# Moving zero fills on VectorE in a decode block: two attention sum banks behind six products, the output accumulator ahead of the layer norm

## Chip, cores, metric

The kernel runs on one core of a Trainium2 chip. The metric is device time in microseconds (us). Runs are compared with runs of the kernel before on the same chip.

## The reference, cut to what matters

Four sequences, one new token each, width 640. A layer norm feeds two branches that are added to x: attention over the last 2048 positions of a cache with 32 heads of 192, and a gated feed-forward of width 1536.

```python
xn = layernorm(x)
q = xn @ wq                                         # 640 -> 32 x 192
k, v = k_cache[:, :, Sk - W:], v_cache[:, :, Sk - W:]   # W = 2048
p = softmax(q . k * 192 ** -0.5)
attn = (p . v) @ wo
ffn = (silu(xn @ w1) * (xn @ w3)) @ w2
return x + attn + ffn
```

Each element of the cache is used once: 32 K heads and 32 V heads of 3 MB each (3.146 million bytes) are 201 of the 223 MB that are read.

## The kernel before

Positions lie on the partitions. VectorE multiplies a quarter of a K head by q (a "product", `mult`), TensorE sums pieces of it into PSUM (`adder`), VectorE finishes the sum (`reduce_quarter`), and after four quarters a softmax and the product with V (`pv`) follow. K has two buffers and V three; a load is issued when the last user of its buffer is done.

```python
# query projection: two rounds of six PSUM banks, evacuated to qbc
for c0 in range(0, NQ, 6):
    qps = [pool.tile([P, QC], FP32, tag=tag, name="qps")
           for pool, tag in ((ps_add, "ps"), (ps_add, "ps"), (ps_o, "o_ps"), (ps_o, "o_ps"), (ps_m, "mt"), (ps_t, "t"))]
    ...                                   # matmuls, copies by ScalarE, in round one also VectorE

o_banks = []                              # the same two banks, now for the sums with V
for i in range(2):
    o_ps = ps_o.tile([P, 2 * Dh], FP32, tag="o_ps", name="o_ps")
    nc.vector.memset(o_ps[:], 0.0)
    o_banks.append(o_ps)
acc = ps_acc.tile([P, N0], FP32, name="acc")
nc.vector.memset(acc[:], 0.0)
...
def mult(u):                              # quarter g of head h
    h, g = u // GQ, u % GQ
    pr = ppool.tile([P, JQ, Dh], BF16, tag="pr")
    nc.vector.tensor_tensor(out=pr[:], in0=kts[h][:, g * JQ:(g + 1) * JQ, :],
                            in1=qbc[:, h * Dh:(h + 1) * Dh].unsqueeze(1).to_broadcast([P, JQ, Dh]), op=ALU.mult)
...
for h in range(H):                        # slots of the hand-made schedule; add(slot, phase, what)
    if h >= KBUFS:
        add((h - KBUFS + 1) * GQ, 0, load_k, h)
    for u in range(u0, ul + 1):
        add(u, 1, mult, u)
        add(u + 1, 2, adder, u)
        add(u + 1, 8, reduce_quarter, u)
    ...
```

## Time and profile before

| | before |
|---|---|
| median of three runs | 525.47 us (525.42 to 525.69) |
| profiled span | 523.7 us |
| busy: TensorE, VectorE, ScalarE | 69%, 65%, 11% |
| transfers | 222.96 MB read, the 16 engines busy 99.3% |
| first product; third K load issued | 33.24 us; 42.47 us |

The prediction shows the lines for this. One more view belongs to it, the waits of the queue's sequencer (who waited for whom: us in total, times, longest):

```profile
SPq L140 <- DVE pr L292: 316.1, 30, 13.1
SPq L140 <- DMA kt<-in_A_k_cache_dram: 72.4, 25, 5.6
```

A K load waits for VectorE's last product on the same buffer.

### The profile page before, as it was taken

To read this page: it belongs to the slowest core of one execution; us is meant where nothing else is said; L and a number is where in the kernel's file an instruction comes from. 1 tells how busy PE (TensorE), PEld (TensorE's weight loads), DVE (VectorE), ACT (ScalarE), POOL (GpSimd) and SP (SyncE) were. 2 spreads that over 40 slices of the span, in tenths; PEclk is the share of its full clock that TensorE was granted. 3 is DMA by queue.
4 is the path that set the end of the run, shared out by engine and by line. 5 is a ranking of instruction groups with operands and counts; after the bars stand their busy time and mean duration, and the time that the engine had idled before them with its cause. 6 is when DMAs were issued, how large, how long until landed. Compare 5 with 4: busy or idle time off the path is not lost.

```text
span 523.7 us, 4813 instructions
## 1 busy us (share of the span) xinstructions
PE 358.9 (69%) x2337; PEld 74.5 (14%) x1643; DVE 339.2 (65%) x410; ACT 57.3 (11%) x179; POOL 5.6 (1%) x12
## 2 busy tenths in 40 slices
PE   0976756887658776757557768576686876655785
PEld 0100111121111111111111111111111111111122
DVE  3248953687656767577647877467666867667671
ACT  2121111111001110110000111001101100001111
POOL 4000000000000000000000000000000000000000
PEclk9989986898788988799987988799878888999889
DMA  9999999999999999999999999999999999999996
GB/s 391 420 443 421 435 431 428 437 427 429 431 435 428 433 424 445 422 434 432 434 432 433 428 435 434 430 429 432 431 435 432 429 435 430 433 432 429 435 422 276
DMA packets 11904, 223.26 MB, mean 426 GB/s; under 512 B 1332, under 2 KB 1608, under 8 KB 3052
## 3 DMA queue, kind: packets, MB, share of 16 engines
q1 hardware_dynamic: 11868, 222.96, 99.3%
q8 instruction: 15, 0.25, 0.2%
q14 instruction: 5, 0.04, 0.0%
q10 hardware_dynamic: 16, 0.01, 0.0%
HBM read 222.96 MB, written 0.01 MB: 426 GB/s over the span
## 4 chain that ended last, share of the span: by engine, by line
DMA 60%; PE 19%; DVE 15%; ACT 3%; issue 2%; SPq 1%; DVEq 0%
DMA kt<-in_A_k_cache_dram 44%; PE ps L303 11%; DMA w<-in_B_w_dram 10%; DVE pr L292 10%; DMA vt<-in_A_v_cache_dram 5%; PE po L376 4%; DVE sc L311 2%; PE qps L258 2%; ACT ex L339 1%; DVE z L347 1%; DMA x_sb<-in_A_x_dram 1%; PE mt L333 1%; ACT L339 0%; ACT negm L336 0%; PE mt L320 0%
## 5 line engine op out<-in xcount | busy, mean ns | idle before, releaser
L303 PE MATMUL ps<-pr,idb 128*128 128x512 bf16 x768 | 217.3, 426 | 140.5 <-DVE pr L292 140.5
L292 DVE TENSOR_TENSOR pr<-kt,qbc 128x3072 bf16<-128x3072 bf16 x128 | 223.5, 1747 | 101.2 <-DMA kt<-in_A_k_cache_dram 101.2
L311 DVE TENSOR_REDUCE sc<-ps 128x16 f32<-128x512 f32 x128 | 87.1, 681 | 2.7 <-PE ps L303 2.7
L355 PE MATMUL o_ps<-vt,z 128*8 128x384 bf16 x1024 | 53.4, 345 | 0.2 <-DVE z L347 0.2
L376 PE MATMUL po<-o_sb,sel_w 128*32 128x192 f32 x128 | 49.2, 518 | 0.6 <-ACT o_sb L358 0.6
L347 DVE TENSOR_TENSOR z<-ex,mask_b 128x256 bf16<-128x256 bf16 x32 | 13.5, 423 | 41.3 <-ACT ex L339 41.3
L355 PEld LDWEIGHTS <-z 128*8 128x8 bf16 x1024 | 24.5, 89 | 95.2 <-issue 83.5
L358 ACT COPY o_sb<-o_ps 128x384 f32<-128x384 f32 x32 | 15.3, 479 | 189.6 <-PE o_ps L355 189.6
L328 ACT ACTIVATE gneg<-gmax 1x128 f32<-1x128 f32 x32 | 9.8, 308 | 164.6 <-DVE gmax L325 164.6
L320 PEld LDWEIGHTS mt<-idf,lmax 128*1 128x1 f32 x32 | 3.4, 105 | 132.1 <-issue 131.1
L376 PEld LDWEIGHTS po<-o_sb,sel_w 128*32 128x32 f32 x128 | 13.9, 131 | 30.0 <-issue 28.8
L303 PEld LDWEIGHTS <-idb 128*128 128x128 bf16 x124 | 12.0, 96 | 37.7 <-issue 31.6
L333 PEld LDWEIGHTS mt<-ones_ff,gneg 1*128 1x128 f32 x64 | 9.6, 186 | 47.9 <-issue 44.5
L258 PE MATMUL qps<-wt,xnT 128*128 128x512 bf16 x60 | 16.2, 438 | 0.0
L336 ACT COPY negm<-mt 128x1 f32<-128x1 f32 x32 | 5.1, 159 | 72.4 <-PE mt L333 72.4
L333 PE MATMUL mt<-ones_ff,gneg 1*128 1x1 f32 x64 | 12.3, 259 | 0.7 <-ACT gneg L328 0.7
L325 DVE TENSOR_REDUCE gmax<-mt 1x4 f32<-1x128 f32 x32 | 8.8, 275 | 6.0 <-PE mt L320 5.7
L363 PEld LDWEIGHTS po<-rsum,tot_w 128*32 128x32 f32 x64 | 4.4, 108 | 51.0 <-ACT ex L339 34.7
L320 PE MATMUL mt<-idf,lmax 128*1 128x128 f32 x32 | 11.3, 353 | 0.0
L339 ACT ACTIVATE ex<-sc,negm 128x64 bf16<-128x64 f32 x32 | 11.1, 348 | 1.0
L279 PE MATMUL acc<-wo_t,oT 128*4 128x320 bf16 x96 | 9.2, 298 | 1.3 <-DMA wo_t<-in_A_wo_dram 1.3
L214 PE MATMUL xnT_ps<-idb,xn 4*128 4x4 bf16 x5 | 0.4, 178 | 13.5 <-DVE xn L209 13.5
(74 smaller groups left out, 78.7 us busy)
## 6 DMA issues: line engine op xcount, KB each, us to landing
kt<-in_A_k_cache_dram SPq DMA_DIRECT2D x32, 3072.0 KB, 19.0
vt<-in_A_v_cache_dram SPq DMA_DIRECT2D x32, 3072.0 KB, 26.1
wo_t<-in_A_wo_dram SPq DMA_DIRECT2D x8, 960.0 KB, 20.8
wt<-in_A_wq_dram SPq DMA_DIRECT2D x2, 3072.0 KB
w<-in_B_w_dram SPq DMA_DIRECT2D x1, 1920.0 KB
wt<-in_A_wq_dram SPq DMA_DIRECT2D x1, 1536.0 KB, 19.5
w<-in_B_w_dram SPq DMA_DIRECT2D x1, 1536.0 KB
w<-in_B_w_dram SPq DMA_DIRECT2D x2, 640.0 KB
```

The lines of the kernel that those rows point to most:

```text
L258: nc.tensor.matmul(qp[:], lhsT=xnT[:, kc].rearrange("p a b -> p (a b)"), rhs=wq_rows[kc][:, (c0 + i) * QC:(c0 + i + 1) * QC], start=(kc == ...
L292: nc.vector.tensor_tensor(out=pr[:], in0=kts[h][:, g * JQ:(g + 1) * JQ, :], in1=qbc[:, h * Dh:(h + 1) * Dh].unsqueeze(1).to_broadcast([P, ...
L303: nc.tensor.matmul(ps[:], lhsT=idb[:], rhs=pr[:, :, kk * DD:(kk + 1) * DD], start=(kk == 0), stop=(kk == NK - 1))
L311: nc.vector.tensor_reduce(out=scs[h][:, g * JQ:(g + 1) * JQ], in_=pss.pop(u)[:], axis=AX.X, op=ALU.add)
L320: nc.tensor.transpose(out=mt[0:1, 0:P], in_=chs[h][0][:], identity=idf[:])
L328: nc.scalar.activation(out=gneg[:], in_=gmax[:].unsqueeze(1).to_broadcast([1, PB, B]), func=ACTF.Copy, scale=-SCALE)
L333: nc.tensor.matmul(mt[:, P:P + 1], lhsT=gneg[:].rearrange("o p b -> o (p b)"), rhs=ones_ff[:], start=True, stop=True)
L339: nc.scalar.activation(out=ex[:], in_=scs.pop(h)[:], func=ACTF.Exp, bias=negm[:, 0:1], scale=SCALE, accum_out=rsum[:])
L347: nc.vector.tensor_tensor(out=z[:], in0=ex[:].unsqueeze(2).to_broadcast([P, NJ, B]), in1=mask_b[:].unsqueeze(1).to_broadcast([P, NJ, B]), ...
L355: nc.tensor.matmul(o_ps[c * CT:c * CT + 2 * B, :], lhsT=z[:, 2 * jj:2 * jj + 2, :], rhs=vt[:, 2 * jj:2 * jj + 2, :], start=(jj < 4), stop= ...
L358: nc.scalar.copy(out=o_sb[:], in_=o_ps[:])
L376: nc.tensor.matmul(po[sl, 0:Dh], lhsT=sel_w[:, par].rearrange("p a b -> p (a b)"), rhs=o_sb[:, par * Dh:(par + 1) * Dh].rearrange("p (r i) ...
```

## The change

Its intent is to let the first product start as soon as its K head is there: the bank fills must wait until ScalarE has emptied the banks of the query projection, and in VectorE's order everything stood behind that wait.

```diff
+    acc = ps_acc.tile([P, N0], FP32, name="acc")        # ahead of the layer norm
+    nc.vector.memset(acc[:], 0.0)
+
     xf = ppool.tile([B, D], FP32, tag="pr")
...
     o_banks = []
-    for i in range(2):
-        o_ps = ps_o.tile([P, 2 * Dh], FP32, tag="o_ps", name="o_ps")
-        nc.vector.memset(o_ps[:], 0.0)
-        o_banks.append(o_ps)
-
-    acc = ps_acc.tile([P, N0], FP32, name="acc")
-    nc.vector.memset(acc[:], 0.0)
+
+    def o_zero():
+        for i in range(2):
+            o_ps = ps_o.tile([P, 2 * Dh], FP32, tag="o_ps", name="o_ps")
+            nc.vector.memset(o_ps[:], 0.0)
+            o_banks.append(o_ps)
...
+    add(5, 9, o_zero)
```

In the built program slot 5, phase 9 puts the bank fills behind the sixth product and the reduction after it.

## The prediction

> **What bounds the kernel now.** I read the page's busy shares and its 40 slices first, then the queue's waits by who released them, the stretches by stage, the chain of waits, and last the start of the program instruction by instruction, since all three fills lie there.
>
> From the page of the kernel before:
>
> ```profile
> PE 358.9 (69%) x2337; PEld 74.5 (14%) x1643; DVE 339.2 (65%) x410; ACT 57.3 (11%) x179; POOL 5.6 (1%) x12
> ...
> DMA  9999999999999999999999999999999999999996
> ...
> q1 hardware_dynamic: 11868, 222.96, 99.3%
> ...
> HBM read 222.96 MB, written 0.01 MB: 426 GB/s over the span
> ...
> DMA 60%; PE 19%; DVE 15%; ACT 3%; issue 2%; SPq 1%; DVEq 0%
> ```
>
> The reader is to see that no compute engine is above 69%, while the 16 transfer engines are busy in every slice but the last. The stretches by stage (busy times per engine, then granted clock, DMA share, GB/s) say the same of every stage:
>
> ```profile
> 0.00:2.00 2.00, 0.00 (x0) 0.00 (x0) 0.16 (x2) 0.61 (x1) 1.29 (x9) 1.00 0.71 184
> 2.00:26.00 24.00, 11.86 (x53) 1.74 (x24) 8.60 (x27) 4.54 (x8) 4.34 (x4) 1.00 0.99 427
> 26.00:54.00 28.00, 17.85 (x74) 1.20 (x12) 19.19 (x21) 5.23 (x11) 0.00 (x0) 0.94 1.00 428
> 54.00:110.00 56.00, 40.52 (x281) 8.46 (x211) 33.88 (x39) 7.70 (x19) 0.00 (x0) 0.85 1.01 432
> 110.00:484.00 374.00, 260.62 (x1711) 54.82 (x1216) 255.75 (x295) 34.67 (x125) 0.00 (x0) 0.90 1.00 432
> 484.00:518.00 34.00, 26.28 (x203) 7.30 (x162) 20.82 (x29) 4.16 (x15) 0.00 (x0) 0.90 0.99 425
> ```
>
> 222.96 MB at 429 GB/s, the mean of these stages, is 519.7 us; the last loads land at 519.4 to 520.5 and some 3 us of last products, copies and store follow. So the time is bytes over rate plus a short tail. The chain's "DVE 15%" and "PE 19%" are no contradiction: it steps through a product because a K load is issued when the product frees its buffer, but at that moment the queue still holds other loads. The wait of the queue's sequencer for products, 316.1 us in 30 pieces, is therefore waiting with work in the queue.
>
> **The start.** From the order of time of the kernel before (start, length, instruction, idle time before it and its releaser):
>
> ```profile
> 27.60 0.54 SPq L147 DMA_DIRECT2D vt<-in_A_v_cache_dram  x1
> ...
> 30.41 3.03 ACT L266 CAST qbc<-qps 128x512 bf16<-128x512 f32 x6 [5.11 <-PE qps L258]
> 32.13 0.87 DVE L272 MEMSET o_ps<- 128x384 f32 x2 [6.28 <-ACT qbc L266]
> 33.01 0.33 DVE L276 MEMSET acc<- 128x320 f32 x1
> 33.24 3.40 DVE L292 TENSOR_TENSOR pr<-kt,qbc 128x3072 bf16<-128x3072 bf16 x2
> ...
> 42.47 0.54 SPq L140 DMA_DIRECT2D kt<-in_A_k_cache_dram  x1
> ...
> 54.85 1.76 DVE L292 TENSOR_TENSOR pr<-kt,qbc 128x3072 bf16<-128x3072 bf16 x1 [0.53 <-DMA kt<-in_A_k_cache_dram]
> ```
>
> VectorE idles 6.28 us before the fills: they reuse two banks of the query projection, so they wait for ScalarE to empty these. The first product stands behind them in order. The third K load (42.47) follows the fourth product, which empties the first K buffer. The first product of that third K head starts at 54.85, after a wait for its data.
>
> **What the Trainium skill says.** "VectorE: DVE Perf Modes", section "Zero memsets can be issued as uint32 (trn2)", gives a memset one cycle per element, and the page's specifications 0.96 GHz: 400 ns for 384 elements, 333 for 320. The trace agrees roughly: 378 and 325 ns. "PSUM — Partial Sum Buffer", section "PSUM bank collisions raise a hardware error", says that the chip does not arbitrate two engines in one bank, so the wait of the fill for ScalarE is needed; the 6.28 us show the wait, no run shows a collision. "DMA: Bandwidth & Descriptors", section "Where 436 GB/s comes from", gives 435 GB/s for the 16 ports; the trace's steady 432 agrees, so there is hardly rate left to gain. Its section "Queues, rings and completion order" says that each engine consumes descriptors in ring order: a K load that is issued earlier goes behind what is already queued. No view so far shows this directly; the changed kernel will.
>
> **The change, part by part.** Nothing is removed or added; the built program has the same instructions on every engine, in the same order but for three fills on VectorE.
>
> 1. The accumulator's fill (325 ns) goes before the conversion of x, where VectorE idles 3.84 us for x to land. It costs nothing there and takes 0.33 us from between the projection and the first product.
>
> 2. The two bank fills (2 x 0.378 us, 0.87 with the gap) go behind the sixth product and the reduction after it. There their banks have long been emptied, so they wait for nothing, but they are 0.87 us in a stretch where VectorE is nearly full. The first product of softmax weights with V into these banks is at 55.2, some 5 us later: not endangered.
>
> 3. The larger effect is the wait. The first product needs the first K head and the first 512 columns of q, copied by about 24.3. In the changed program it waits for that load and for ScalarE directly. I take the latter to mean that first copy and not the last one: before, the product had no wait of its own for ScalarE beyond the fills', which cover only the copies out of their two banks, and ScalarE's sixth copy ended at 33.44, after the product had begun. When does the K head land? It is behind 7.86 MB of projection weights: 11.0 MB in all. The first 26 us move 0.37 + 10.25 = 10.6 MB, so its last bytes go at about 27, and a landing trails that count by some 2 us (the second K head, 14.2 MB, would be due at 34.3 and has 32.8 us from issue to landing, about 35.2). So the first product starts at 27 to 29, not at 33.24.
>
> From there TensorE bounds the gain: its projection runs to 31.45 and the first adder (six matmuls, 1.46 us at full clock) follows it. Estimated: adder 31.5 to 33.0, reduction 33.1, third product 33.8, second reduction 35.5, fourth product 36.1 to 37.8. The third K load is then issued at about 38, some 4.5 us before 42.47. If the clock drop that the trace shows at about 35 to 38 comes earlier, and hits both first adders (2.76 us for six at half clock), this shrinks to some 3 us.
>
> The second K head, landed at about 35.2, doesn't hold this up. The next issue (53.75) comes 4.5 - 0.87, or 3 to 4 us, earlier.
>
> 4. What that is worth. By 42.47, 19.07 MB had been issued and about 10.6 + 16.47 us x 0.428 = 17.7 MB moved: 1.4 MB, or 3.2 us, was still queued. It is the thinnest point I find, but the queue was not dry. The third K head's last bytes are at 22.2 MB, due at about 53 whenever it is issued, as long as the queue doesn't run dry. So VectorE arrives at its first product some 3.5 us earlier and waits that much longer: the 0.53 us of wait before 54.85 becomes about 4. There the gain ends. All later times are those of the bytes.
>
> What can remain: in single microseconds the share falls to 0.75 at 41 to 42, just ahead of the late issue. From 41 to 42.5 the trace moves 344, 295 and 393 GB/s in half microseconds against 428: 0.5 x (84 + 133 + 35) = 126, over 428, is 0.3 us. An earlier issue may fill this, and it moves every later landing by as much. Sum: 525.47 - 0.0 to 0.3; I take 525.3.
>
> **The rivals.** (a) The start is on the path and the whole gain of some 4 us reaches the end: 521.5 us. For it speaks the chain of waits, which runs through these fills and products; against it the 1.00 share from 26 to 54 us, since 4 us fewer would need 429 to become 432.5 GB/s over the whole run. (b) The wait for ScalarE only changes its owner: the product now carries the wait itself, and if it covers all query copies it starts at 33.5, where it did before. The time is then 525.5, and only the 0.87 us of fills behind the sixth product remain as a loss, hidden by the wait for the third K head. Against it speaks the start at 33.24 before ScalarE's end. (c) The products run beside the projection and its copies and slow them, or the fills delay the second head's softmax and its V buffer's release. VectorE would have to lose over 3 us to let the queue run dry; nothing so long is in the change, and a loss of 1 us would give 526. (d) The shift brings the short-packet loads of the first feed-forward weight into another phase and costs or saves a few tenths, 525.0 to 525.9.
>
> **Range and chances.** Three runs lie within 0.27 us. With 0 to 0.3 us of gain, a few tenths for phases and as much for another chip, 524.5 to 526.1 should hold the time 8 times in 10. A change of 2% is 10.5 us, more than double of all that the start's idle time can give, and more than the 6.28 us of the wait itself: 1% for faster. For slower an unseen wait of 10 us would have to arise: 1%. Within 2%: 98%.
>
> **What would show it.** Right: the first product at 27 to 29 with no fills before it; two fills of 0.38 us after the reduction behind the sixth product; the third K load issued at 38 to 39.5; the wait of the product at about 54.5 grown to 3 to 4 us; total bytes and mean rate as before (426 to 427 GB/s). Wrong: a first product at 33 (rival b); a third K head that lands 3 us sooner, and with it an end several us earlier (rival a), which would mean that the queue was emptier at 42 than I counted; or a share under 0.9 in any slice where it was 1.

## The result and the profile after

The changed kernel took 525.68 us (median of six, 525.53 to 525.77), the kernel before 525.46 (525.41 to 525.69). The ratio is 1.0003 with a 95% interval of 0.9991 to 1.0016: the same. (A ratio is the mean time of one kernel's runs over that of the other's of the same rounds, so not quite the ratio of the medians quoted.)

Lines of the page after, which answer to the first fence of the prediction:

```profile
PE 358.8 (69%) x2336; PEld 75.4 (14%) x1643; DVE 339.1 (65%) x410; ACT 57.3 (11%) x179; POOL 5.6 (1%) x12
...
DMA  9999999999999999999999999999999999999996
...
q1 hardware_dynamic: 11868, 222.96, 99.3%
...
HBM read 222.96 MB, written 0.01 MB: 426 GB/s over the span
...
DMA 68%; PE 16%; DVE 13%; ACT 2%; issue 0%; SPq 0%; DVEq 0%
```

And of the stretches by stage (last two columns: share of the transfer engines and GB/s):

```profile
26.00:54.00 28.00, 17.75 (x105) 1.88 (x44) 19.20 (x20) 5.70 (x12) 0.00 (x0) 1.00 1.00 428
...
110.00:484.00 374.00, 262.63 (x1712) 55.69 (x1216) 256.17 (x296) 34.65 (x125) 0.00 (x0) 0.90 1.01 432
```

Busy times, bytes and rates stand still. In the chain only the shares move, 8 points from engines to transfers: the same span, told as waiting for data. The start, in order of time after:

```profile
26.30 0.54 SPq L147 DMA_DIRECT2D vt<-in_A_v_cache_dram  x1
...
28.30 3.43 DVE L295 TENSOR_TENSOR pr<-kt,qbc 128x3072 bf16<-128x3072 bf16 x2 [3.76 <-DMA kt<-in_A_k_cache_dram]
...
29.11 3.04 ACT L269 CAST qbc<-qps 128x512 bf16<-128x512 f32 x6 [5.11 <-PE qps L261]
...
36.29 0.54 SPq L140 DMA_DIRECT2D kt<-in_A_k_cache_dram  x1
...
41.91 0.79 DVE L277 MEMSET o_ps<- 128x384 f32 x2
...
47.56 0.55 SPq L140 DMA_DIRECT2D kt<-in_A_k_cache_dram  x1
...
55.28 1.76 DVE L295 TENSOR_TENSOR pr<-kt,qbc 128x3072 bf16<-128x3072 bf16 x1 [7.14 <-DMA kt<-in_A_k_cache_dram]
```

The first product starts at 28.30 us instead of 33.24, and what it waited for is its K head, no longer ScalarE, whose second round of query copies begins only at 29.11. The third K load is issued 6.2 us earlier (36.29 for 42.47), the fourth also (47.56 for 53.75). Then VectorE comes to the first product of the third head and waits 7.14 us for the data, where before it waited 0.53. That product starts at 55.28, before at 54.85. All that was won is waited away here, 55 us into the program. At the next load it has even turned round, in the traces before and after:

```profile
64.81 0.54 SPq L140 DMA_DIRECT2D kt<-in_A_k_cache_dram  x1
...
67.19 0.55 SPq L140 DMA_DIRECT2D kt<-in_A_k_cache_dram  x1
```

The fifth K load is issued 2.4 us later than before. The granted clock was 0.50 from 56 to 62 us, just behind 6.64 us in which TensorE had waited, where before it was 1.00; the six matmuls behind the third head's first product took 2.72 us instead of 1.46. That the waiting brought the low clock is my reading; no run tests it. By the sixth K load, at 90.24 for 90.09, the shift is gone.

### The profile page after: what moved, and what is told of

Its sections match the earlier page's. It is cut to its first block, busy times and chain, and to the rows that moved or that the text cites. A ratio compares the mean times of both kernels' runs of the same rounds, so it can differ in the third digit from the quotient of the medians.

```text
span 523.5 us, 4813 instructions
## 1 busy us (share of the span) xinstructions
PE 358.8 (69%) x2336; PEld 75.4 (14%) x1643; DVE 339.1 (65%) x410; ACT 57.3 (11%) x179; POOL 5.6 (1%) x12
## 3 DMA queue, kind: packets, MB, share of 16 engines
q1 hardware_dynamic: 11868, 222.96, 99.3%
HBM read 222.96 MB, written 0.01 MB: 426 GB/s over the span
## 4 chain that ended last, share of the span: by engine, by line
DMA 68%; PE 16%; DVE 13%; ACT 2%; issue 0%; SPq 0%; DVEq 0%
DMA kt<-in_A_k_cache_dram 53%; DMA w<-in_B_w_dram 11%; PE ps L306 10%; DVE pr L295 10%; DMA vt<-in_A_v_cache_dram 5%; PE po L379 4%; DVE sc L314 2%; ACT ex L342 1%; DVE z L350 1%; PE mt L336 1%; PE mt L323 0%; ACT negm L339 0%; PE f_ps L430 0%; PE o_ps L358 0%; PE acc L282 0%
## 5 line engine op out<-in xcount | busy, mean ns | idle before, releaser
L306 PE MATMUL ps<-pr,idb 128*128 128x512 bf16 x768 | 214.4, 421 | 140.0 <-DVE pr L295 140.0
L358 PE MATMUL o_ps<-vt,z 128*8 128x384 bf16 x1024 | 57.9, 367 | 0.2 <-DVE z L350 0.2
L358 PEld LDWEIGHTS <-z 128*8 128x8 bf16 x1024 | 25.6, 93 | 96.6 <-issue 86.5
L361 ACT COPY o_sb<-o_ps 128x384 f32<-128x384 f32 x32 | 15.3, 478 | 194.1 <-PE o_ps L358 194.1
L261 PE MATMUL qps<-wt,xnT 128*128 128x512 bf16 x59 | 14.6, 406 | 0.1
```

The source lines that it names most:

```text
L261: nc.tensor.matmul(qp[:], lhsT=xnT[:, kc].rearrange("p a b -> p (a b)"), rhs=wq_rows[kc][:, (c0 + i) * QC:(c0 + i + 1) * QC], start=(kc == ...
L306: nc.tensor.matmul(ps[:], lhsT=idb[:], rhs=pr[:, :, kk * DD:(kk + 1) * DD], start=(kk == 0), stop=(kk == NK - 1))
L358: nc.tensor.matmul(o_ps[c * CT:c * CT + 2 * B, :], lhsT=z[:, 2 * jj:2 * jj + 2, :], rhs=vt[:, 2 * jj:2 * jj + 2, :], start=(jj < 4), stop= ...
L361: nc.scalar.copy(out=o_sb[:], in_=o_ps[:])
```

## The experiments

All eleven kernels passed the comparison with the reference, also the two that are wrong: one wrong V head, or two wrong groups of the output weight, are within its tolerance, which makes them no more right.

### The change again, and its two parts

First the change once more in five rounds, because the 0.2 us between the medians has the wrong sign.

> The changed kernel once more, five rounds beside the kernel before on one chip, to see whether the 0.2 us by which it was slower is there. Theory (bytes over rate set the end; the start's gain is waited away at the third K head): ratio 0.9995 to 1.0010, either sign. Rival (the two fills behind the sixth product cost something real): a steady 1.0005 or more. First product again at 28 to 29 us, third K load issued at 36 to 38, wait before the first product of the third K head 5 to 7 us.

Measured: 525.63 us against 525.53, ratio 1.0003 (0.9990 to 1.0015). First product at 28.33, third K load at 36.80, wait 6.38 us, fifth K load at 66.38.

Then the parts alone. The accumulator's fill:

```diff
+    acc = ps_acc.tile([P, N0], FP32, name="acc")
+    nc.vector.memset(acc[:], 0.0)
     xf = ppool.tile([B, D], FP32, tag="pr")
 ...
-    acc = ps_acc.tile([P, N0], FP32, name="acc")       # behind the bank fills (comment mine)
-    nc.vector.memset(acc[:], 0.0)
```

> Only the accumulator's fill moved, the bank fills stay ahead of the first product. Theory: the first product starts some 0.3 us earlier than before (33.24), at about 32.9, the third K load is issued at about 42, the end is as before: ratio 0.999 to 1.001. Rival (start on the path): 0.3 us or more off the end.

Measured: 525.80 us, ratio 1.0005 (0.9993 to 1.0018). First product at 32.41 (0.5 of the 0.8 us is a query projection that happened to run earlier: VectorE's first copy of it starts at 23.46 for 23.96), third K load at 41.64, wait 1.23 us, fifth K load at 65.47.

The bank fills alone (`o_zero` in slot 5 as in the change, the accumulator's fill left where it was):

> Only the two bank fills moved; the accumulator's fill stays ahead of the first product. Theory: this part carries the whole shift; the accumulator's fill ends while VectorE would be waiting for the first K head anyway, so the first product starts at 28 to 29 and the third K load is issued at 36 to 38, as with both parts; the end is as before: ratio 0.999 to 1.001. Rival (start on the path): some 4 to 6 us off the end.

Measured: 525.54 us, ratio 1.0000 (0.9988 to 1.0013). VectorE in order of time:

```profile
25.13 0.33 DVE L272 MEMSET acc<- 128x320 f32 x1
28.22 3.43 DVE L295 TENSOR_TENSOR pr<-kt,qbc 128x3072 bf16<-128x3072 bf16 x2 [2.76 <-DMA kt<-in_A_k_cache_dram]
```

So the bank fills carry the whole shift: third K load at 36.66, wait 6.55 us, fifth K load at 66.41. The accumulator's fill doesn't matter beside it, since it fits into the wait for the K head. Neither part moves the end by a resolved amount. The 0.2 us stays unresolved: over both series the changed kernel has a mean of 525.69 (11 runs), the kernel before 525.55 (15 runs), with intervals that hold 1 and single runs of the kernel before from 525.29 to 525.87.

One trace of this series shows where a few tenths can come from. The chain that ended last in the repeat of the change:

```profile
478.83 18.03 DMA kt<-in_A_k_cache_dram
...
498.70 2.72 PE ps L306 x6
```

In the first traces of both kernels the end waited for the last weights, due at 520.2 to 520.5. Here it ran through the last K head's own computation, with six matmuls in 2.72 us where full clock takes 1.46. The two ends lie within half a microsecond of each other, so the clock that is granted in the last 25 us may decide which is later. This is a reading of single traces; no run tests it.

### How late may a K load be issued?

If the queue sets the time, a delay of VectorE must be free as long as transfers are queued, and cost its full length afterwards; and the changed kernel must bear more of it. So extra fills of the accumulator, which nothing uses, go between the first and the second product, in both kernels:

```diff
+    def stall():
+        for _ in range(24):                 # also 48 and 12 (comment mine)
+            nc.vector.memset(acc[:], 0.0)
...
             add(u, 1, mult, u)
+            if u == 0:
+                add(u, 1, stall)
```

> The kernel before with 24 more fills of the accumulator on VectorE (about 0.34 us each, 8.2 us) between the first and the second product; nothing uses them. Theory (a queue that holds 3.2 us of transfers at 42.5, when the third K load is issued): the load is issued at about 50, the queue runs dry for some 4 to 5 us and the end comes 4 to 5.5 us later, ratio 1.008 to 1.010. Rival (start on the path): the whole 8 us, 1.0155. Rival (the transfers have ample slack everywhere): nothing.

> The same 24 fills in the changed kernel. Theory: there the third K load was issued at 36.3 with about 9.4 us of transfers queued; 8 us later it is issued at about 44.5, just before the queue would run dry: end 0 to 1 us later, ratio 1.000 to 1.002. Rival (start on the path): the whole 8 us again.

> 48 fills, about 16.4 us, in the kernel before. Theory: 16.4 less 3.2 of slack (some of the fills hide in VectorE's wait for the first adder): end 12 to 13.5 us later, ratio 1.023 to 1.026, with a gap in the transfers of that length. Rival (start on the path): 16.4 us.

> 48 fills in the changed kernel. Theory: 16.4 less 9.4 of slack: end 6 to 7.5 us later, ratio 1.011 to 1.014; the difference to the kernel before with the same fills is the slack that the change bought, about 6 us. Rival (start on the path): 16.4 us later, no difference between the two.

My length for the fills was wrong: a fill has a row of 325 ns, but 24 of them took 11.06 us and 48 took 22.26, 0.46 us each. All delays were thus a third longer than expected, and the expected times were missed: 533.99 us (+8.4) with 24 fills in the kernel before, 529.61 (+4.0) in the changed one, 544.87 (+19.3) and 540.92 (+15.3) with 48. Ratios: 1.0158, 1.0077, 1.0374, 1.0291. With 24 fills the kernel before even hit the figure of the rival (1.0155). That is a coincidence of lengths: the load was issued 10.3 us later, not 8, and the changed kernel lost only half as much. With the lengths that the traces show the theory can still be tried, and it gives the cost. The stretches from 44 to 54 us, with 24 fills, in the kernel before:

```profile
44.00:46.00 2.00, 0.00 (x0) 0.00 (x0) 1.44 (x5) 0.00 (x0) 0.00 (x0) 0.50 0.90 373
46.00:48.00 2.00, 0.38 (x2) 0.00 (x0) 2.00 (x2) 0.00 (x0) 0.00 (x0) 0.50 0.11 39
48.00:50.00 2.00, 2.00 (x6) 0.00 (x0) 1.76 (x2) 0.00 (x0) 0.00 (x0) 0.50 0.00 0
50.00:52.00 2.00, 2.00 (x7) 0.00 (x0) 1.63 (x2) 0.00 (x0) 0.00 (x0) 0.75 0.00 0
52.00:54.00 2.00, 1.24 (x7) 0.00 (x0) 2.00 (x3) 0.00 (x0) 0.00 (x0) 1.00 0.00 0
```

and in the changed kernel:

```profile
44.00:46.00 2.00, 2.00 (x6) 0.00 (x0) 1.39 (x2) 0.00 (x0) 0.00 (x0) 0.50 0.88 366
46.00:48.00 2.00, 2.00 (x6) 0.00 (x0) 1.97 (x2) 0.00 (x0) 0.00 (x0) 0.50 0.09 34
48.00:50.00 2.00, 1.77 (x7) 0.00 (x0) 1.82 (x2) 0.00 (x0) 0.00 (x0) 0.84 0.74 197
50.00:52.00 2.00, 1.41 (x7) 0.18 (x2) 1.97 (x4) 0.00 (x0) 0.00 (x0) 1.00 0.63 270
52.00:54.00 2.00, 1.04 (x7) 0.00 (x0) 1.92 (x4) 0.31 (x1) 0.00 (x0) 1.00 1.20 516
```

In both, what had been issued runs out at about 46.2 us, and the transfers stop until the third K load, issued at 52.76 and 48.00, delivers. (The view counts a transfer packet where it starts.) Counted as bytes that were not moved at 430 GB/s: before, 2 x (373 + 39) = 824 of 4300, so 3476 over 430 = 8.1 us; changed, 2 x (366 + 34 + 197 + 270 + 516) = 2766, so 3.6 us. The ends came 8.4 and 4.0 us later. To within half a microsecond the time lost is the time in which the queue was empty.

With 12 fills, the length now known, a second pair was to show a delay that only the changed kernel bears for nothing.

> The kernel before with 12 fills between the first and the second product; in the earlier runs such a fill took 0.46 us, not 0.34, so 5.5 us. In all four of those runs what had been issued ran out at 46.2 us, and the first bytes of the third K head came some 1.2 us after its issue. Theory: here the issue moves from 42.5 to about 47.2, the first bytes to 48.4, the queue is dry for 2 to 3 us, and the end comes 2 to 3 us later: ratio 1.004 to 1.006. Rival (start on the path): 4.7 us or more, 1.009.

> The same 12 fills in the changed kernel. Theory: the issue moves from 36.3-36.8 to about 42.5, where the kernel before has it without fills; its first bytes are wanted at 46.2 at the earliest, so nothing runs dry: ratio 0.9995 to 1.0015, although VectorE works 5.5 us longer. Rival (the start is on the path in this kernel too): 1.009.

Measured: the kernel before 528.34 us, ratio 1.0053 (1.0040 to 1.0065); the changed kernel 526.04 us, ratio 1.0007 (0.9995 to 1.0020). The issues and the stretch that tells them apart, first the kernel before:

```profile
46.48 0.54 SPq L140 DMA_DIRECT2D kt<-in_A_k_cache_dram  x1
...
46.00:48.00 2.00, 1.96 (x8) 0.00 (x0) 1.81 (x3) 0.00 (x0) 0.00 (x0) 0.89 0.48 124
```

then the changed one:

```profile
41.53 0.54 SPq L140 DMA_DIRECT2D kt<-in_A_k_cache_dram  x1
...
46.00:48.00 2.00, 1.22 (x6) 0.00 (x0) 1.90 (x4) 0.31 (x1) 0.00 (x0) 1.00 1.18 505
```

Put together (shift of the issue against the same kernel without fills; bytes missing at 430 GB/s counted as above, from 44 to 54 us for 12 and 24 fills and from 42 to 68 us for 48; end against the kernel before on the same chip):

| kernel | fills | third K load | shift | missing | end later | shift less end |
|---|---|---|---|---|---|---|
| before | 12 | 46.48 | 4.0 | 2.5 | 2.7 | 1.3 |
| before | 24 | 52.76 | 10.3 | 8.1 | 8.4 | 1.9 |
| before | 48 | 64.32 | 21.9 | 20.3 | 19.3 | 2.6 |
| changed | 12 | 41.53 | 5.2 | 0 | 0.4 | 4.8 |
| changed | 24 | 48.00 | 11.7 | 3.6 | 4.0 | 7.7 |
| changed | 48 | 59.28 | 23.0 | 14.9 | 15.3 | 7.7 |

The last column is the margin: the kernel before bore a delay of 1 to 2 us free of charge, the changed one 7.7 (with 12 fills it wasn't used up). The issues and the missing bytes are of one profiled run, the ends are medians. For 48 fills in the kernel before, the profiled run was the slowest of four (546.78 us, 21.2 later): with its own end the margin of that row is 0.7 and not 2.6, and the loss is no shorter than the gap; the rows with 12 and 24 fills become 1.0 and 1.4. The shifts also lean on one trace per kernel (36.29; the repeat had 36.80, which makes 7.7 into 7.2). Without that: the issue less the later end is 43.8, 44.4 and 45.0 us in the kernel before, 44.0 and 44.0 in the changed one. Both kernels have the same deadline for this load, some 44 to 45 us after the start; the one meets it with 1 to 2 us to spare, the other with 7 to 8.

At this load the change bought some 6 us of margin, the amount by which it moved the issue, and no time, because nothing in the kernel spends it. At the fifth load it took some margin away, by the issues above; no run measured how much is there. That the start is on the path, the rival with 4 us of gain, is refuted: it needs the same loss in both kernels with every delay.

### Are the bytes the price?

The other half of the theory: fewer bytes must pay at the rate of the transfers. First the changed kernel without one V load:

```diff
-        if h < H - 2:
+        if h < H - 2 and h != 12:
             add(u0 + 2, 0, load_v, h)
...
-        o_ps, z, vt = o_banks[h % 2], zs.pop(h), vts.pop(h)
+        o_ps, z, vt = o_banks[h % 2], zs.pop(h), (vts[h] if h == 11 else vts.pop(11 if h == 12 else h))
```

> The changed kernel without the V load of head 12, which uses the V of head 11 (wrong result on purpose); every engine's work is the same. Theory: 3.146 MB fewer at 432 GB/s are 7.3 us: 518.2 to 518.6, ratio about 0.986. Rival (the chain of products and softmax sets the time): no change, ratio above 0.995.

Measured: 520.68 us (four runs), ratio 0.9911 (0.9896 to 0.9927): 4.9 us less, not 7.3. The expectation missed by a third. The trace shows a hole where the load is missing:

```profile
224.00:226.00 2.00, 1.00 (x4) 0.00 (x0) 1.62 (x3) 0.00 (x0) 0.00 (x0) 0.84 0.63 270
226.00:228.00 2.00, 2.00 (x16) 0.30 (x16) 0.00 (x0) 0.00 (x0) 0.00 (x0) 0.50 0.81 295
```

2 x (430 - 270) + 2 x (430 - 295) = 590, over 430, is 1.4 us. Without this load only one K load was queued there, and it ran low before VectorE released the next buffer. So the margin in the middle of the kernel is below the 7.3 us that one head takes. About 1 us of the difference has no row that I could name.

A second try takes smaller pieces away, at two places:

```diff
-        add(hg * HG * GQ + 8, 0, wo_load, hg)
+        if hg not in (2, 4):
+            add(hg * HG * GQ + 8, 0, wo_load, hg)
...
-        oT, wo_t = oTs[hg], wos[hg]
+        oT, wo_t = oTs[hg], wos[hg - 1 if hg in (2, 4) else hg]
```

> The changed kernel without two of the eight loads of the output weight (960 KB each, groups 2 and 4, which use the weights of groups 1 and 3; wrong result on purpose). They are 1.966 MB: 4.55 us at 432 GB/s. Each thins the queue by 2.3 us only, where the missing V load thinned it by 7.3 and let it run short. Theory: no shortage, the full 4.3 to 4.6 us: ratio 0.9912 to 0.9918. Rival (the bytes are not the price, part of the time is elsewhere): two thirds of it, as the missing V load gave, 3 us, 0.994.

Measured: 521.38 us against 525.60, ratio 0.9918 (0.9905 to 0.9932): 4.2 us less, and the page counts 220.99 MB at 426 GB/s over the span, the same rate as before:

```profile
HBM read 220.99 MB, written 0.01 MB: 426 GB/s over the span
```

That is 4.2 of the 4.55 us that 1.97 MB take at 432 GB/s; the interval, 3.6 to 5.0 us, holds the full price. Four-microsecond stretches from 60 to 340 us show no hole: none is under 0.94. The rival's 0.994 is outside the interval.

## Why the prediction was right

The number alone would say little: any forecast of no change, rival (b)'s 525.5 too, falls into the range. What was right is the path.

**The bound** (bytes over rate, then a short tail) held: same bytes, same 428 and 432 GB/s, same end, and taking 1.97 MB away gave 4.2 us. **Part 1**, the accumulator's fill, cost nothing, as said; alone it brought the first product to 32.41. **Part 2**, the bank fills, took 0.79 us at 41.91. They cost even less than said: from the third to the fourth K load it is 11.28 us before and 11.27 after, since they lie in a stretch in which VectorE waits for ScalarE's exponentials anyway (1.35 us before, 0.50 after). **Part 3**: the first product at 27 to 29 us for its K head and not for ScalarE's last copy came out at 28.30, which refutes rival (b). **Part 4**, the wait that takes the gain, is the step that the prediction stands on, and it was there, at the product that was named: a load issued 6.2 us earlier went behind what was already queued, and landed no earlier.

Sizes were off in three terms, and two readings of lines were not sound:

- The third K load was predicted at about 38 and issued at 36.29; the wait predicted at about 4 us was 7.14. I had taken the projection's end, 31.45, from one trace. In the trace after, the first adder starts at 30.12; VectorE's first query copy started anywhere from 22.66 to 24.50 in the traces here, with no relation to the fills. That is 1.3 of the 1.7 us. The fourth K load keeps the whole shift of 6.2 us, because the 0.87 us that I took off for the fills was not lost; with the 0.53 us of wait from before, and data that landed 0.4 us later, this makes the 7.14.
- The transfers still queued at 42.47, estimated at 3.2 us, proved to be 3.7 (they ran out at 46.2), but the usable margin only 1 to 2, because the first bytes come 1.3 us after a load's issue began. The estimate left that out.
- The gain of 0 to 0.3 us from the dip at 41 to 42 was not found: in none of the four series of the change and its parts is a difference resolved from zero, and the medians lean the other way. The prediction's middle, 525.3, was low by 0.4. The dip itself was no sign of missing transfers: half-microsecond counts swing that much anywhere, 590 GB/s just before it (40 to 40.5 us), and 737 and then 98 GB/s in the trace after (39 to 40 us).
- The 429 GB/s is the plain mean of five stages. Weighted by their lengths it is 431, and 222.96 MB take 517.2 us; the slow first 2 us (184 GB/s) and the thinner end make up the rest to 519.4 to 520.5.
- A landing was said to trail the byte count by some 2 us; the example beside it gives 0.9 (35.2 less 34.3). With that the first product was due at 27.8 and came at 28.30. The range of 27 to 29 held, with that much luck.

Rival (a) fell with the first trace and, as an experiment, with the delays. Rival (c) is not seen in the time, and no slice's share fell, though VectorE came later to the fifth load. Rival (d), a few tenths either way for phases, can be neither shown nor excluded at this noise.

## What to carry to other kernels

When the transfers are busy all the time, ask of every earlier issue how much was queued at that moment: that margin, not the length of the wait, says what the issue is worth. The margin can be measured in one pair of runs by delaying the engine that releases the buffer until the end moves; up to there the delay is free, beyond it it costs its full length. What comes out is a deadline for the load; here it was the same before and after the change. A change that only widens the margin, and does so at every load, is worth keeping for the day when something else uses it, but it is not a speed-up, and the wait that disappears in one place is to be looked for at the next load's data.

## What the Trainium skill lacked or had wrong

- "DMA: Bandwidth & Descriptors", section "Specifications", gives a first-byte latency of about 0.6 us for this kind of queue, without saying from which moment. With an empty queue the first packet started 1.3 us after the start of the issue (52.76 to 54.09, 48.00 to 49.33, 64.32 to 65.66 us), 0.8 after its end.
- The same page's section "Where 436 GB/s comes from" says that about 358 GB/s bind a transfer from HBM, without saying there that this is the share of a core whose neighbour also streams; the page does say so further up, in "Measured". This kernel, on one core, read HBM at 432 GB/s for 374 us; the 435 of the ports is the figure that fits.
- "VectorE: DVE Perf Modes", section "The DRAIN you can't avoid", says, of a chain of copies, that the semaphore after each costs nothing extra. Fills of one tile, each waiting for the one before, came every 0.46 us with rows of 325 ns; the product behind the accumulator's fill, which doesn't wait for it, started 0.23 us after it (33.01 and 33.24). Whether the semaphore costs this or the fill of the same tile, no run separates.
- No page that I read tells how to find how late a load may be issued: 1 to 2 us before the change, 7.7 after it.
